# Query, key and leftover-row events of a fused attention and expert kernel, moved to other steps, and one of four row copies dropped

## The chip, the cores and the metric

One core of one Trainium2 chip runs the whole program in one launch. The metric is the device time of that core in microseconds (us). Three runs of the kernel before took 1332.02, 1334.98 and 1339.14 us; the median is 1334.98.

## The reference, cut to what matters

```python
def sm(a, b):                       # softmax of scale * a @ b.T over the last axis
    ...
a2k = sm(agents, k); agent_v = a2k @ v          # 49 agents, 4 batches of 11456 tokens, 128 wide
q2a = sm(q, agents); x = q2a @ agent_v          # one row per token
logits = x @ w_gate; expert_idx = argmax(logits)
gate_w = softmax(logits)[expert_idx]
for e in range(8):                              # 128 -> 1024 -> 128
    out[mask_e] = gate_w * (relu(x[mask_e] @ w1[e]) @ w2[e])
```

All inputs and the output are float32.

## The kernel before, in words

The four batches go one after the other. A batch has 11 chunks of 1024 tokens and one of 192, and every chunk has two groups of 512 tokens (the last one has one), 23 groups in all. For each batch the expert that most tokens choose is computed for all tokens, densely: 23 groups times 8 slices of the 1024 hidden values are 184 **steps**. The tokens of other experts are done in gathered blocks, late in the last batch and behind it.

A token's row x is never formed in the dense part. x is E times AV, with E the 49 exponentials of the token and AV the 49 agent values, so the first layer is E times (AV times w1). `esplit` (lines 581 to 588) writes each E as float16 parts into 128 columns of `mm`: 49 high parts, 49 low parts (E minus the high part), and the first 30 high parts once more. `eturn` (L593) turns that by a DMA transpose issued by SyncE into M, where those 128 columns are partitions. The weights W (L734) hold, for the first 98 rows, the high part of AV times w1, and for the last 30 rows its low part. 19 low-part rows (E 30 to 48) don't fit into 128; `rest` (L602) copies the 19 high-part partitions 30 to 48 of M four times into the tile Q, at partitions 0, 32, 64 and 96, and the weights Wq hold their low parts at the same places. A step of the first layer is thus two matmuls into one PSUM bank: L1190 (19 rows, from Q; four steps' worth are issued together, one per group of partitions) and L1198 (128 rows, from M). ScalarE then takes the relu in float16 (L1203) and VectorE its low part (L1204), and five steps later TensorE does the second layer, 12 matmuls a step (L1217). After the eighth slice VectorE scales the group by its factor (L1230, tile yo), and SyncE stores it.

The order of work is written out by a planner. `at(t, f)` puts a call at a time t in steps (`base` is 184 times the batch) and `after(dt, f)` puts one dt behind the present one; all calls are made in the order of these times, and each engine's instructions are in the order in which the calls made them. Nothing waits for the time itself; an engine that is ahead goes on. So the times set the order within each engine's queue, SyncE's (SP's) DMA queue among them, and waits come from data and buffers alone. The names that the change touches:

- Keys: chunk c of a batch is loaded, squared (L321), scaled and split into two float16 parts (L337, L339) from time `ks + 10 c` with ks = -208, its scores come 9 steps later. For batch 1 that is step -24 of batch 0 for c = 0. `KS1` is a list of such times for batch 1 alone, empty before.
- Queries: chunk c starts at `QA + 8 c` for c below 3 and then every 13 steps (`QC`; 10.5 in the last batch), with QA = -20. Batch 0's chunks have times of their own (`QS0`, `Q0`). Scores (`qscores`) follow 9 steps later (`KL`; 11 in the last batch from chunk 3), with the exponentials (`qexp`, L578); `esplit` 3 steps after the scores, `eturn` 0.5 after that (`DTE`), `rest` 3.5 after the turn (`DTQ`); `logits` (L610, the gate's logits, read from M) `LL` = 9.5 steps after the scores (`LLL` = 11 in the last batch).
- Each chunk c is used by the first layer from step 16 c on. M has 6 buffers, Q 3, yo 3, and a split key or query has two transposed buffers (hT, L361).
- Stores: `DEX` = 2 is the delay of the store of the exponentials behind `qexp`, `DST` = 2 that of the store of yo behind L1230.

Of the kernel before, what the change touches and what calls it, by code (L numbers as in the profile page):

```python
# [17 lines left out]
ALU = mybir.AluOpType  # L18
# [4 lines left out]
A = 49  # L23
KR = 128 - 2 * A
CH = 1024
BIG = float(1 << 20)
# [22 lines left out]
KS, KT, VT, VL, VL4, TW0, TW1, DW = -208, 10, 4, 4, 4, 8, 2.5, 1  # L49
QA, QB, QC, QB3, KL, LL, RG, D1, DL = -20, 8, 13, 10.5, 9, 9.5, 0.7, 0.5, 0  # L50

KS1 = []

KLL, LLL = 11, 11

DTR, DTE, DTQ, DEX, DST, DXS = 2, 0.5, 3.5, 2, 2, 0.5

# [13 lines left out]
def agent_moe_kernel(ctx, tc, q, k, v, agents, wg, w1, w2, out):  # L71
# [52 lines left out]
    nc.gpsimd.iota(itmp[:, 0:1], pattern=[[0, 1]], base=0, channel_multiplier=1)  # L124
    nc.vector.tensor_copy(pidx, itmp[:, 0:1])
    sumrow = cpool.tile([P, 1], F32, name="sumrow")
    nc.vector.tensor_scalar(sumrow, pidx, float(2 * A), None, op0=ALU.is_lt)
    restrow = cpool.tile([P, 1], F32, name="restrow")
    nc.vector.tensor_scalar(restrow, pidx, float(2 * A), None, op0=ALU.is_ge)
    eidx = cpool.tile([P, E], F32, name="eidx")  # L130
# [129 lines left out]
    def attention(b):  # L260
# [227 lines left out]
        def agentvalues(i):  # L488
# [10 lines left out]
            elif i == 2:  # L499
# [4 lines left out]
                nc.tensor.matmul(pt[:, :A], AV["acc"][:64 + A], both[:64 + A], start=True, stop=True)  # L504
                nc.vector.tensor_tensor(av[:, :2 * A].rearrange("p (j a) -> p j a", a=A), pt[:, :A].unsqueeze(1).broadcast_to([P, 2, A]),
                                        rs.unsqueeze(1).broadcast_to([P, 2, A]), op=ALU.mult)
                nc.vector.tensor_copy(av[:, 2 * A:], av[:, :KR])
                avq = one.tile([P, 4, 32], F32, tag="avq", name="avq")
# [72 lines left out]
        def esplit(c):  # L581
            _, p, t = chunks[c]
            e, m2 = Es[c], mm[c % len(mm)]
            nc.vector.tensor_copy(m2[:p, :t, :A], e[:p, :t, :])  # L584
            nc.scalar.copy(m2[:p, :t, 2 * A:], e[:p, :t, :KR])
            eng = nc.gpsimd if pick(M2L if last else M2E, c) == "P" else nc.vector
            eng.tensor_tensor(m2[:p, :t, A:2 * A], e[:p, :t, :], m2[:p, :t, :A], op=ALU.subtract)  # L587
            after(0 if first and c == 0 else DTE, eturn, c, m2)

        def eturn(c, m2):  # L590
            _, p, t = chunks[c]
            m = mpool.tile([P, 8, P], F16, tag="M", name="M")
            nc.sync.dma_start_transpose(m[:, :t, :p], m2[:p, :t, :].rearrange("p t a -> p (t a)"))  # L593
            Ms[c] = m
            after(0 if first and c == 0 else DTQ, rest, c)

        def rest(c):

            _, p, t = chunks[c]
            x = Qs[c] = mpool.tile([P, 8, P], F16, tag="Q", name="Q", bufs=MQ)  # L600
            for r in range(4):
                nc.sync.dma_start(x[32 * r:32 * r + A - KR, :t, :p], Ms[c][KR:A, :t, :p])  # L602

# [191 lines left out]
        for c in range(NCK):  # L795
# [11 lines left out]
            tl = max(t + ql_ + (TL if first and c < NQ else LLL if last and c > 2 else LL), ta + (TLM if first else 4) + c / 2)  # L807
            at(base + tl, logits, c)
            if c + 1 in starts or c == NCK - 1:
                turns(route(c), base + tl + 1, RG, 6)  # L810
# [364 lines left out]
    def experts(b):  # L1175
# [7 lines left out]
        def rests(g, f0):  # L1183
# [3 lines left out]
            for r in range(4):  # L1187
                k = slice(32 * r, 32 * r + A - KR)
                ph = phs[g, f0 + r] = psH.tile([P, 512], F32, tag="h", name="ph")
                nc.tensor.matmul(ph[:, :nn], st['Wq'][k, f0 // 4, :], st['Q'][c][k, h:h + n, :chunks[c][1]], start=True, stop=False)  # L1190

# [174 lines left out]
```

## Time and profile before

| | |
|---|---|
| runs, median (lowest to highest) | 1334.98 us (1332.02 to 1339.14) |
| profiled execution | 1331.0 us, span 1329.3 us |
| mean granted TensorE clock | 0.889 |
| TensorE (PE) busy | 1066.8 us, 80% of the span |
| VectorE (DVE) busy | 993.6 us, 75% |
| ScalarE (ACT) busy | 767.5 us, 58% |
| GpSimd (POOL) busy | 141.7 us, 11% |
| DMA queue of SP and ACT | 267792 packets, 192.36 MB, 63.5% of 16 engines' span |

The span is the time from the first to the last instruction of the profiled execution. Busy shares are means over the start (0 to 112 us), four batches of dense steps (112 to 1268 us) and the gathered blocks behind them. Weight loads (PEld) overlap matmuls. A granted clock of 1.0 is 2.4 GHz, of 0.5 it is 1.2 GHz.

### The profile page before, as it was taken

The page shows a single profiled execution, that of the slowest core. Times are in us where ns is not written, and L with a number is a line of the kernel's source. Part 1 is how long each engine was busy: PE and PEld are TensorE (multiplying, and loading weights), DVE is VectorE, ACT ScalarE, POOL GpSimd, SP SyncE. Part 2 cuts the span into 40 slices and gives each one's busy share as a digit, 9 for nine tenths or more (in the row PEclk, how much of TensorE's full clock was granted, in tenths as well). Part 3 has the DMA queues.
Part 4 walks back from the last instruction along what each step waited for, and adds up shares of the span by engine and source line. Part 5 has one row for each costly group of instructions (what it writes and reads, how often), then busy time and mean ns, then how long its engine had stood idle before and what let it go on. Part 6 is the DMA issues. An engine that isn't in the chain of part 4 may idle for free. (4 is left out here: it accounts for less than half of the span.)

```text
span 1329.3 us, 35044 instructions
## 1 busy us (share of the span) xinstructions
PE 1066.8 (80%) x14238; PEld 831.8 (63%) x14238; DVE 993.6 (75%) x2454; ACT 767.5 (58%) x1393; POOL 141.7 (11%) x198
## 2 busy tenths in 40 slices
PE   8626779789978668789987759779987859989995
PEld 8514657667765456567765547567765637666795
DVE  3677857678887768388886858497886957988975
ACT  4457745565586655365495745365483535665582
POOL 0200000032000000030200000030200102210123
PEclk9767988889988879799988988899987979888998
DMA  8679998643398999553298999733275456444170
GB/s 320 208 168 202 221 198 149 101 134 78 114 252 159 187 188 162 144 144 81 92 268 152 175 206 129 182 101 79 90 175 83 75 128 141 88 136 133 52 245 15
DMA packets 269813, 197.94 MB, mean 149 GB/s; under 512 B 218313, under 2 KB 231106, under 8 KB 269648
## 3 DMA queue, kind: packets, MB, share of 16 engines
q1 hardware_dynamic: 267792, 192.36, 63.5%
q0 software_dynamic: 1568, 2.25, 0.9%
q8 instruction: 113, 1.85, 0.6%
q10 hardware_dynamic: 288, 1.05, 0.2%
q14 instruction: 52, 0.43, 0.1%
HBM read 99.75 MB, written 36.43 MB: 102 GB/s over the span
## 5 line engine op out<-in xcount | busy, mean ns | idle before, releaser
L1217 PE MATMUL py<-w2h,hh 128*128 128x128 f16 (+1 forms) x5760 | 612.8, 230 | 31.1 <-DVE yo L1230 23.3
L1217 PEld LDWEIGHTS <-hh 128*128 128x128 f16 x8640 | 571.3, 104 | 102.7 <-issue 45.8
L1204 DVE SCALAR_TENSOR_TENSOR hh<-ph,hh 128x512 f16<-128x512 f32 (+1 forms) x736 | 479.3, 668 | 157.0 <-ACT hh L1203 152.9
L1203 ACT ACTIVATE hh<-ph 128x512 f16<-128x512 f32 (+1 forms) x728 | 405.5, 585 | 329.3 <-PE ph L1198 231.1
L1217 PE MATMUL py<-w2l,hh 128*128 128x128 f16 (+1 forms) x2880 | 554.3, 230 | 0.0
L1198 PE MATMUL ph<-M,W 128*128 128x512 f16 (+1 forms) x736 | 267.5, 397 | 0.0
L1190 PE MATMUL ph<-Q,Wq 19*128 19x512 f16 (+1 forms) x736 | 114.8, 399 | 67.3 <-DVE hh L1204 55.5
L1198 PEld LDWEIGHTS <-W 128*128 128x128 f16 x736 | 66.8, 99 | 126.5 <-issue 120.0
L321 ACT ACTIVATE jk<-ld 128x1024 f16<-128x1024 f32 (+1 forms) x84 | 84.7, 1009 | 49.0 <-DMA ld<-in_q_dram 37.7
L339 DVE SCALAR_TENSOR_TENSOR hl<-ld,mul,hl 128x1024 f16<-128x1024 f32 (+1 forms) x84 | 102.5, 1225 | 11.4 <-ACT hl L337 11.2
L337 ACT ACTIVATE hl<-ld,mul 128x1024 f16<-128x1024 f32 (+1 forms) x84 | 90.2, 1100 | 27.6 <-DVE mul L206 14.9
L610 PE MATMUL ps_small<-Gs,M 128*128 128x18 f16 x360 | 16.9, 173 | 95.5 <-DMA M<-mm 94.3
L388 PE MATMUL ps_small<-agh,hT 128*128 128x49 f16 (+1 forms) x630 | 64.6, 192 | 22.5 <-DMA hT<-hl 22.3
L587 POOL TENSOR_TENSOR mm<-E,mm 128x392 f16<-128x392 f32 (+1 forms) x18 | 15.6, 868 | 623.8 <-DVE mm L584 472.7
L610 PEld LDWEIGHTS <-M 128*128 128x128 f16 x360 | 13.6, 100 | 101.9 <-DMA M<-mm 100.0
L388 PEld LDWEIGHTS <-hT 128*128 128x128 f16 (+1 forms) x630 | 56.9, 102 | 27.3 <-DMA hT<-hl 23.3
L1190 PEld LDWEIGHTS <-Wq 19*128 19x128 f16 x736 | 25.6, 92 | 66.9 <-issue 50.3
L1230 DVE TENSOR_TENSOR yo<-py,cs 128x512 f32<-128x512 f32 (+1 forms) x92 | 61.4, 667 | 5.4 <-PE py L1217 5.3
L389 PE MATMUL ps_small<-agl,hT 128*128 128x49 f16 (+1 forms) x630 | 63.9, 191 | 0.0
L390 PE MATMUL ps_small<-agh,hT 128*128 128x49 f16 (+1 forms) x630 | 63.8, 191 | 0.0
L389 PEld LDWEIGHTS <-hT 128*128 128x128 f16 (+1 forms) x630 | 56.1, 102 | 7.2 <-issue 5.0
L390 PEld LDWEIGHTS <-hT 128*128 128x128 f16 (+1 forms) x630 | 55.4, 102 | 0.0
(295 smaller groups left out, 1309.7 us busy)
## 6 DMA issues: line engine op xcount, KB each, us to landing
ld<-in_k_dram SPq DMA_DIRECT2D x44, 512.0 KB
ld<-in_v_dram SPq DMA_DIRECT2D x44, 512.0 KB
ld<-in_q_dram SPq DMA_DIRECT2D x44, 512.0 KB
out_dram<-yo SPq DMA_DIRECT2D x88, 256.0 KB
w1e<-in_moe_w_dram SPq DMA_DIRECT2D x17, 512.0 KB
w2e<-in_moe_w_dram SPq DMA_DIRECT2D x17, 512.0 KB
exps<-E SPq DMA_DIRECT2D x44, 196.0 KB
wn<-in_moe_w_dram SPq DMA_DIRECT2D x16, 512.0 KB
```

What stands on the lines that cost most here:

```text
L321: nc.scalar.activation(jk[:p, :t * D], x[:p, :t, :].rearrange("p t d -> p (t d)"), AF.Square, accum_out=ss[:p])
L337: nc.scalar.activation(hi[:p, :t, :], x[:p, :t, :], AF.Copy, scale=m)
L339: nc.vector.scalar_tensor_tensor(lo[:p, :t, :], x[:p, :t, :], m, hi[:p, :t, :], op0=ALU.mult, op1=ALU.subtract)
L388: nc.tensor.matmul(o, x[:, 0, i, :p], AG["h"], start=True, stop=False)
L389: nc.tensor.matmul(o, x[:, 0, i, :p], AG["l"], start=False, stop=False)
L390: nc.tensor.matmul(o, x[:, 1, i, :p], AG["h"], start=False, stop=True)
L1190: nc.tensor.matmul(ph[:, :nn], st['Wq'][k, f0 // 4, :], st['Q'][c][k, h:h + n, :chunks[c][1]], start=True, stop=False)
L1198: nc.tensor.matmul(ph[:, :nn], st['W'][:, f, :], st['M'][c][:, h:h + n, :chunks[c][1]], start=False, stop=True)
L1203: nc.scalar.activation(hh[:, 0, :nn], ph[:, :nn], AF.Relu)
L1204: nc.vector.scalar_tensor_tensor(hh[:, 1, :nn], ph[:, :nn], 0.0, hh[:, 0, :nn], op0=ALU.max, op1=ALU.subtract)
L1217: mm_ = lambda l, r, **k: nc.tensor.matmul(o, l, r, skip_group_check=True, **k)
L1230: nc.vector.tensor_tensor(yo[:p, :n, :], py[:p, :n * D].rearrange("p (i d) -> p i d", d=D), cs.unsqueeze(2).broadcast_to([p, n, D]), op=AL ...
```

## The change

- The 128 columns of `mm` are laid out anew: 49 low parts, the first 17 high parts, all 49 high parts (columns 66 to 114), and 13 more high parts (17 to 29). The high parts 30 to 48 thus lie at partitions 96 to 114 of M. `av`, the row masks and the two ScalarE casts of `esplit` follow that layout.
- `rest` makes three copies in place of four, from partitions 96 to 114; the fourth of the L1190 matmuls reads M there. `rest` is no longer called behind `eturn` but from the plan, at `16 c - QD` with QD = 9, or at 6.5 steps behind the scores if that is later.
- QA goes from -20 to -26, LL from 9.5 to 14, LLL from 11 to 15; DEX from 2 to 4 and DST from 2 to 5.
- Batch 1's keys have times of their own: chunk c at step 3 + 7.6 c of batch 0.

```diff
--- before.py
+++ after.py
@@ -22,6 +22,8 @@
 P = 128
 A = 49
 KR = 128 - 2 * A
+UP = 96 - KR
+DUP = ((A, 0, UP - A), (UP + A, UP - A, KR))
 CH = 1024
 BIG = float(1 << 20)
 UNROLL = 4
@@ -47,13 +49,13 @@
 VE, T1, TF0, TF1, TL, TLM, Q0 = 12, 1.75, 3, 1.5, 18, 10, 2
 
 KS, KT, VT, VL, VL4, TW0, TW1, DW = -208, 10, 4, 4, 4, 8, 2.5, 1
-QA, QB, QC, QB3, KL, LL, RG, D1, DL = -20, 8, 13, 10.5, 9, 9.5, 0.7, 0.5, 0
-
-KS1 = []
-
-KLL, LLL = 11, 11
-
-DTR, DTE, DTQ, DEX, DST, DXS = 2, 0.5, 3.5, 2, 2, 0.5
+QA, QB, QC, QB3, KL, LL, RG, D1, DL = -26, 8, 13, 10.5, 9, 14, 0.7, 0.5, 0
+
+KS1 = [3 + 7.6 * c for c in range(12)]
+
+KLL, LLL = 11, 15
+
+DTR, DTE, QD, DEX, DST, DXS = 2, 0.5, 9, 4, 5, 0.5
 
 LAG = 5
 
@@ -123,10 +125,14 @@
     pidx = cpool.tile([P, 1], F32, name="pidx")
     nc.gpsimd.iota(itmp[:, 0:1], pattern=[[0, 1]], base=0, channel_multiplier=1)
     nc.vector.tensor_copy(pidx, itmp[:, 0:1])
+    restrow = cpool.tile([P, 1], F32, name="restrow")
+    for o, a0, a1 in DUP:
+        nc.vector.tensor_scalar(itmp[:, 1:2].bitcast(F32), pidx, float(o), None, op0=ALU.is_ge)
+        nc.vector.tensor_scalar(itmp[:, 2:3].bitcast(F32), pidx, float(o + a1 - a0), None, op0=ALU.is_ge)
+        nc.vector.tensor_tensor(itmp[:, 3 + (a0 > 0):4 + (a0 > 0)].bitcast(F32), itmp[:, 1:2].bitcast(F32), itmp[:, 2:3].bitcast(F32), op=ALU.subtract)
+    nc.vector.tensor_tensor(restrow, itmp[:, 3:4].bitcast(F32), itmp[:, 4:5].bitcast(F32), op=ALU.add)
     sumrow = cpool.tile([P, 1], F32, name="sumrow")
-    nc.vector.tensor_scalar(sumrow, pidx, float(2 * A), None, op0=ALU.is_lt)
-    restrow = cpool.tile([P, 1], F32, name="restrow")
-    nc.vector.tensor_scalar(restrow, pidx, float(2 * A), None, op0=ALU.is_ge)
+    nc.vector.tensor_scalar(sumrow, restrow, -1.0, 1.0, op0=ALU.mult, op1=ALU.add)
     eidx = cpool.tile([P, E], F32, name="eidx")
     itmp2 = cpool.tile([P, E], I32, name="itmp2")
     nc.gpsimd.iota(itmp2, pattern=[[1, E]], base=0, channel_multiplier=0)
@@ -502,9 +508,10 @@
                 av = wpool.tile([P, P], F32, tag="av", name="av")
                 pt = small_ps()
                 nc.tensor.matmul(pt[:, :A], AV["acc"][:64 + A], both[:64 + A], start=True, stop=True)
-                nc.vector.tensor_tensor(av[:, :2 * A].rearrange("p (j a) -> p j a", a=A), pt[:, :A].unsqueeze(1).broadcast_to([P, 2, A]),
-                                        rs.unsqueeze(1).broadcast_to([P, 2, A]), op=ALU.mult)
-                nc.vector.tensor_copy(av[:, 2 * A:], av[:, :KR])
+                nc.vector.tensor_tensor(av[:, :A], pt[:, :A], rs, op=ALU.mult)
+                nc.vector.tensor_copy(av[:, UP:UP + A], av[:, :A])
+                for o, a0, a1 in DUP:
+                    nc.vector.tensor_copy(av[:, o:o + a1 - a0], av[:, a0:a1])
                 avq = one.tile([P, 4, 32], F32, tag="avq", name="avq")
                 nc.gpsimd.memset(avq, 0.0)
                 nc.gpsimd.tensor_copy(avq[:, :, :A - KR], av[:, KR:A].unsqueeze(1).broadcast_to([P, 4, A - KR]))
@@ -581,10 +588,12 @@
         def esplit(c):
             _, p, t = chunks[c]
             e, m2 = Es[c], mm[c % len(mm)]
-            nc.vector.tensor_copy(m2[:p, :t, :A], e[:p, :t, :])
-            nc.scalar.copy(m2[:p, :t, 2 * A:], e[:p, :t, :KR])
+            up = m2[:p, :t, UP:UP + A]
+            nc.vector.tensor_copy(up, e[:p, :t, :])
+            for o, a0, a1 in DUP:
+                nc.scalar.copy(m2[:p, :t, o:o + a1 - a0], e[:p, :t, a0:a1])
             eng = nc.gpsimd if pick(M2L if last else M2E, c) == "P" else nc.vector
-            eng.tensor_tensor(m2[:p, :t, A:2 * A], e[:p, :t, :], m2[:p, :t, :A], op=ALU.subtract)
+            eng.tensor_tensor(m2[:p, :t, :A], e[:p, :t, :], up, op=ALU.subtract)
             after(0 if first and c == 0 else DTE, eturn, c, m2)
 
         def eturn(c, m2):
@@ -592,14 +601,13 @@
             m = mpool.tile([P, 8, P], F16, tag="M", name="M")
             nc.sync.dma_start_transpose(m[:, :t, :p], m2[:p, :t, :].rearrange("p t a -> p (t a)"))
             Ms[c] = m
-            after(0 if first and c == 0 else DTQ, rest, c)
 
         def rest(c):
 
             _, p, t = chunks[c]
             x = Qs[c] = mpool.tile([P, 8, P], F16, tag="Q", name="Q", bufs=MQ)
-            for r in range(4):
-                nc.sync.dma_start(x[32 * r:32 * r + A - KR, :t, :p], Ms[c][KR:A, :t, :p])
+            for r in range(3):
+                nc.sync.dma_start(x[32 * r:32 * r + A - KR, :t, :p], Ms[c][96:96 + A - KR, :t, :p])
 
         def logits(c):
             _, p, t = chunks[c]
@@ -806,6 +814,7 @@
             at(base + t + ql_ + 3, esplit, c)
             tl = max(t + ql_ + (TL if first and c < NQ else LLL if last and c > 2 else LL), ta + (TLM if first else 4) + c / 2)
             at(base + tl, logits, c)
+            at(base + max(c * 16 - QD, t + ql_ + 6.5), rest, c)
             if c + 1 in starts or c == NCK - 1:
                 turns(route(c), base + tl + 1, RG, 6)
                 tf = max(tl + 1 + 6 * RG, tw + 1)
@@ -1187,7 +1196,8 @@
             for r in range(4):
                 k = slice(32 * r, 32 * r + A - KR)
                 ph = phs[g, f0 + r] = psH.tile([P, 512], F32, tag="h", name="ph")
-                nc.tensor.matmul(ph[:, :nn], st['Wq'][k, f0 // 4, :], st['Q'][c][k, h:h + n, :chunks[c][1]], start=True, stop=False)
+                nc.tensor.matmul(ph[:, :nn], st['Wq'][k, f0 // 4, :], st['Q' if r < 3 else 'M'][c][k, h:h + n, :chunks[c][1]],
+                                 start=True, stop=False)
 
         def layer1(g, f):
             c, h, n = groups[g]
```

## Rows read from the trace of the kernel before

**Rows 1.** Busy time by stretch (us from the span's start and length; busy us of PE, PEld, DVE, ACT and POOL with their instructions; granted clock; DMA share and GB/s). Batch 0's chunks 0 to 6 run from 112 to 295; batch 1's chunks 0 to 7 from 400 to 618 and the rest of it to 701; batch 2's chunks 0 to 7 from 701 to 919.

```profile
112.00:295.00 183.00, 148.45 (x2029) 113.45 (x2026) 133.91 (x282) 111.39 (x204) 16.51 (x15) 0.87 0.83 172
...
400.00:618.00 218.00, 170.66 (x2362) 129.60 (x2362) 159.41 (x362) 127.13 (x233) 16.17 (x17) 0.88 0.77 159
618.00:701.00 83.00, 74.26 (x1015) 57.55 (x1014) 68.86 (x187) 54.17 (x97) 10.90 (x28) 0.96 0.55 155
701.00:919.00 218.00, 169.42 (x2361) 128.90 (x2361) 158.46 (x362) 124.70 (x226) 16.20 (x17) 0.89 0.79 152
```

**Rows 2.** What TensorE waited for between the first and the last step, 112 to 1268 us (us in total, times, longest us).

```profile
PE ps_small L610 <- DMA M<-mm: 86.2, 21, 8.2
PE ph L1190 <- DVE hh L1204: 55.5, 39, 11.3
PE py L1217 <- DVE yo L1230: 23.3, 28, 2.9
PE ph L1190 <- DMA Q<-M: 9.9, 11, 2.0
```

**Rows 3.** TensorE in order of time before the first step (start us, us, instruction, count, and in brackets the idle time before it and what ended it).

```profile
91.78 0.38 PE L610 MATMUL ps_small<-Gs,M 128*128 128x18 f16 x8 [1.05 <-DMA M<-mm]
...
107.80 0.22 PE L388 MATMUL ps_small<-agh,hT 128*128 128x49 f16 x1 [14.95 <-DMA hT<-hl]
...
111.68 0.61 PE L1190 MATMUL ph<-Q,Wq 19*128 19x512 f16 x4
```

**Rows 4.** SP's DMA queue in order of time before the first step (start us, us until the last of the group was issued).

```profile
87.51 2.09 SPq L593 DMA_TRANSPOSE M<-mm  x1
...
90.36 5.58 SPq L602 DMA_DIRECT2D Q<-M  x8
96.04 11.77 SPq L361 DMA_TRANSPOSE hT<-hl  x2
```

**Rows 5.** Groups of instructions by line over the whole span (count, busy us, mean ns of one, idle before).

```profile
L339 DVE SCALAR_TENSOR_TENSOR hl<-ld,mul,hl 128x1024 f16<-128x1024 f32 (+1 forms) x84 | 102.5, 1225 | 11.4 <-ACT hl L337 11.2
L337 ACT ACTIVATE hl<-ld,mul 128x1024 f16<-128x1024 f32 (+1 forms) x84 | 90.2, 1100 | 27.6 <-DVE mul L206 14.9 <-DMA hT<-hl 12.7
L321 ACT ACTIVATE jk<-ld 128x1024 f16<-128x1024 f32 (+1 forms) x84 | 84.7, 1009 | 49.0 <-DMA ld<-in_q_dram 37.7 <-DVE hb L202 6.0 <-DMA ld<-in_k_dram 4.9
```

**Rows 6.** SP's queue in order of time at the start of batch 1.

```profile
396.14 2.53 SPq L602 DMA_DIRECT2D Q<-M  x4
```

**Rows 7.** TensorE in order of time at the start of batch 1, the first-layer lines.

```profile
400.15 0.37 PE L1190 MATMUL ph<-Q,Wq 19*128 19x512 f16 x1 [0.44 <-DMA Q<-M]
...
401.90 0.37 PE L1190 MATMUL ph<-Q,Wq 19*128 19x512 f16 x1 [1.00 <-DMA Q<-M]
...
403.46 0.58 PE L1190 MATMUL ph<-Q,Wq 19*128 19x512 f16 x1 [0.87 <-DMA Q<-M]
```

**Rows 8.** SP's queue in order of time around the transpose of M of batch 1's chunk 4.

```profile
464.09 1.24 SPq L593 DMA_TRANSPOSE M<-mm  x1
465.43 3.76 SPq L361 DMA_TRANSPOSE hT<-hl  x1
469.29 2.46 SPq L602 DMA_DIRECT2D Q<-M  x4
```

**Rows 9.** The first layer's L1198, one matmul a step, from the span's start to 464.09 us: count; shortest, median and longest ns; start of the first and the last; forms. The same 228 stand there up to 468.5 us.

```profile
L1198 PE MATMUL ph<-M,W x228: 243/379/634, 112.2 to 461.0; 128*128 128x512 f16 x110, 128*128 128x192 f16 x4
```

**Rows 10.** TensorE in order of time, the logits of two chunks of batch 1.

```profile
468.76 0.38 PE L610 MATMUL ps_small<-Gs,M 128*128 128x18 f16 x8 [7.37 <-DMA M<-mm]
...
537.37 0.38 PE L610 MATMUL ps_small<-Gs,M 128*128 128x18 f16 x8 [8.22 <-DMA M<-mm]
```

**Rows 11.** What TensorE waited for from 112 to 295 us (batch 0).

```profile
PE ph L1190 <- DVE hh L1204: 15.0, 5, 5.9
PE ps_small L610 <- DMA M<-mm: 11.2, 4, 5.4
PE py L1217 <- DVE yo L1230: 8.1, 6, 2.9
```

**Rows 12.** What TensorE waited for from 400 to 618 us (batch 1).

```profile
PE ps_small L610 <- DMA M<-mm: 30.4, 5, 8.2
PE py L1217 <- DVE yo L1230: 5.1, 4, 2.7
PE ph L1190 <- DVE hh L1204: 4.6, 6, 2.0
```

**Rows 13.** Busy time by short stretches in batch 1, columns as in rows 1. Packets are booked by their start, so a share can pass 1.

```profile
452.00:468.00 16.00, 8.75 (x129) 6.36 (x126) 10.37 (x15) 9.99 (x20) 0.00 (x0) 0.88 0.99 236
468.00:474.00 6.00, 5.24 (x56) 5.24 (x57) 2.22 (x6) 1.79 (x3) 0.00 (x0) 0.50 0.55 137
474.00:494.00 20.00, 13.59 (x217) 10.73 (x215) 15.47 (x32) 12.56 (x22) 0.90 (x1) 0.93 1.08 205
494.00:499.00 5.00, 4.62 (x48) 2.81 (x49) 3.27 (x7) 2.91 (x7) 0.00 (x0) 0.50 0.56 145
```

**Rows 14.** What SP waited for from 400 to 618 us (us in total, times, longest us).

```profile
SPq L602 <- DMA M<-mm: 6.3, 4, 3.3
...
SPq L1293 <- DVE yo L1230: 3.5, 2, 2.5
```

**Rows 15.** The casts of L585 over the whole span (count; shortest, median and longest ns; start of the first and the last; forms).

```profile
L585 ACT CAST mm<-E x48: 230/387/467, 74.8 to 1164.4; 128x240 f16<-128x240 f32 x44, 96x60 f16<-96x60 f32 x4
```

## The prediction, made before the change was run

> **What bounds the kernel now.** I read the stretches first [rows 1]. Steps run at two paces. In the last third of a batch TensorE is busy nearly throughout; in the first two thirds (400 to 618 us for the second batch, 128 steps, so 1.7 us a step) it is busy 171 of 218 us at a mean granted clock of 0.88, VectorE 159, and the DMA engines 0.77 of the time: no engine is full, so something in the order of the work makes holes. The waits of TensorE name it [rows 2]: of its idle time from step 0 to the last step 86.2 us, in 21 waits, go to the logits (L610) for the transposed chunk M; the next ones are 55.5 us for VectorE's hh, 23.3 us for yo, 9.9 us for Q. The third thing to see is the start: TensorE ends the first batch's logits at 92.2 us, and its first layer matmul starts at 111.68 us; the 14.95 us before 107.80 are a wait for a key transpose of the *second* batch, which stands ahead of the first layer in its program [rows 3].
>
> **The change part by part.** The sum is made against the profiled execution, 1331.0 us (span 1329.3); the median of the runs shown is 1334.98, 4 us above it, and I add those 4 us at the end.
>
> *Second batch's keys (KS1).* Key chunks 0, 1 and 2 of batch 1 were due at steps -24, -14 and -4, with scores nine steps later; they are now due at 3, 10.6 and 18.2, so no key stands ahead of the first layer. What is late next? M of chunk 2 is issued at 87.51 to 89.60 [rows 4], its logits start at 91.78 [rows 3], and the first three Q copies, now due at step -9, come behind that transpose on SP. Four copies took 2.53 us to issue at a batch's start [rows 6], so three take 1.9: 89.7 to 91.6. There the first copy's user ran 4.0 us after the issue began (396.14 to 400.15) [rows 6, 7], so the first layer can start near 95.6 instead of 111.7: **-16**. Bounds: -19.5 (straight behind the logits, 92.2) and -10 (the copies stuck behind one more hT transpose: the two at 96.04 held SP 11.77 us, some 6 each).
>
> The three chunks' work now lies beside steps 3 to 30: VectorE 3 x 1.2 for L339, ScalarE 3 x (1.0 + 1.1) for L321 and L337 [rows 5], and three loads and transposes on DMA. At no cost if holes hide it; fully serial it is three hT transposes of about 5.9 us of SP, some 17 us [rows 4]. The first batch's dense stretch already runs at DMA 0.83 [rows 1], so I take a bit under half: **+8**, bounds 0 and +17.
>
> *Queries six steps sooner, logits later (QA, LL, LLL).* QA moves the queries of batches 1 to 3 by -6, LL adds 4.5: logits come 1.5 steps sooner than before, but M's turn (esplit + 0.5) comes 6 sooner, so the lead from M's issue to its use grows from 6 to 10.5 steps. (In batch 0 only the logits move, later.) Example: chunk 4 of batch 1 has M due at step 184 + 34.5; SP issued it at 464.09 [rows 8], when TensorE had done 228 steps [rows 9], 9.5 steps late; it was in use at 468.76, after a wait of 7.37 us [rows 10]. 4.5 steps at the free pace of some 1.2 us are 5.4 us. The longest of the 21 waits are 8.22 and 7.37 [rows 10]; cutting 5.4 from each leaves some 10 us in all, so 76 go. But a wait that goes is not a time that goes. In batch 0's dense stretch M waits are only 11.2 us, and there hh and yo hold TensorE 23.1 us; in batch 1's M holds it 30.4, and those two 9.7 [rows 11, 12]. 19.2 us less of the one goes with 13.4 more of the others, in stretches with different work; I take the nearer middle, 0.6 of 76: **-46**. Bounds 0 (all replaced) and -86 (all gone).
>
> A cross-check by the engine that is fullest there: 0.77 x 218 is 168 us of DMA; packed to 0.87 it would need 193, 25 less in each of batches 1 and 2, with a few more in the others. The same size.
>
> *The clock.* After the wait of 7.37 us that ended at 468.76 [rows 10], the granted clock is 0.50 (1.2 GHz) from 468 to 474, with TensorE busy 5.24 of 6.00 us; from 474 to 494 it is 0.93 [rows 13]. The Trainium skill (TensorE: Matmul & The Clock Gate, "HAM oscillation — how this bites in real kernels") tells of the same: a kernel that waits on DMA in every round of its loop starts each round with a cold array. By that rule the forecast here is too small, since each wait that goes also gives back part of a half-speed stretch. I leave it out of the sum (whoever replaces M may keep the holes), and it is the second rival below.
>
> *Q copies (three, nine steps ahead).* Before, a chunk's four copies were due 3.5 steps after M's issue, and SP stood waiting for M (6.3 us in 400 to 618) [rows 14]. At the three later batch starts Q was due 4 steps ahead; it is now 9: of the 9.9 us of Q waits [rows 2] **-7** (bounds 0, -9.9). At all other chunk starts Q used to be there long before its use; now it has 9 steps, at 1.5 us some 13.5 us. From the first issue to the third group's start took 7.3 us at a batch start (396.14 to 403.46) [rows 6, 7]. So SP may run about 4 steps late before TensorE waits; the example's Q was due at step 222 and issued at 228 [rows 8, 9], 6 late, so 2 steps or 3 us of wait is possible at the worst chunks, numbers 2 to 7 of each batch, 24 in all. I take a seventh of that: **+10**, bounds 0 and +72. The fourth copy's issue, 48 x 0.6 us of SP, goes beside other work: 0 (bounds 0, -5); the fourth group now reads partitions 96 to 114 of M, which its partner matmul reads anyway.
>
> *Stores later (DST, DEX).* SP's waits for yo are short where it is tight, 3.5 us in 400 to 618 [rows 14]; elsewhere nothing urgent stands behind them. 0, bounds -10 and 0; yo has three buffers for one store every eight steps, so five steps of delay fit.
>
> *Layout of the split.* ScalarE's one cast of 240 elements (0.39 us; 60 elements took 0.23) becomes two of 136 and 104: by that line 0.30 + 0.27, so 0.2 more in each of 45 chunks [rows 15], 9 us of an engine busy 127 of 218 [rows 1]; hidden, **+0**, bound +9. Two more small VectorE copies in each batch's av and six more small operations at the program's start, beside the key loads: **+1**, bounds 0 and +3.
>
> Sum: -16 + 8 - 46 - 7 + 10 + 1 = **-50**, 1281 us for the profiled execution, 1285 as a median.
>
> **Rivals.**
> *Given back* (chance 0.18): in the dense stretches DMA or SP is the bound, and M's wait is where it shows. For it: DMA stands at 0.99 to 1.08 (packets booked by their start) at 452 to 468 and 474 to 494; against: it falls to 0.55 between them, right after TensorE's wait for M, and to 0.56 behind them [rows 13]. Then 16 of the start remain, against up to 17 for the three key chunks, and the edges' 7: 0 to -15, 1320 to 1335. The Trainium skill (Perfetto Trace Analysis, "What \"DMA-bound\" means") puts such a bound on the DMA engines or on the issuing sequencer, and only fewer or larger descriptors help it; here that would be one copy in four alone. The holes in the DMA share speak against it.
> *More* (0.10): all M waits go and nothing follows, and the clock stays up: -16 - 86 - 7 and 2.6 us (half of 5.24) [rows 13] after half of the 21 waits, 27: -136 + 8, some 1207.
> *Slower* (0.12): the Q copies come late. The place is L1190 at each chunk's start, where nothing waited before. The 9 steps allow a lag of 4; at M's 9.5 it would cost 5.5 steps, 8 us, in each of 24 chunks, far more than all gains. It turns the change into a loss from 60 us in all, 2.5 us a chunk, a mean lag of near 6 steps, which the example's Q just had. The price I give it is +10 to +30: 1345 to 1365. Against it: a shorter queue lags less, since SP no longer stands for M.
> That the change doesn't do what it says would show at the start alone: if layer 1 still waited there, -16 would be missing; it is within the first rival.
>
> **How the numbers follow.** Forecast (-15 to -90) 0.60, given back 0.18, more 0.10, slower 0.12. A measurement of this kernel can tell about 0.5%, 6.7 us, from no change. Faster by over that: 0.60 + 0.10 + 0.10 of the first rival: 0.80; within it 0.08 of that rival and 0.02 of the last: 0.10; slower 0.10. The range 1245 to 1331 holds the forecast and most of the first rival and leaves out the last and most of "more", some 0.2.
>
> **What would show it.** Start: the first L1190 at 93 to 98 us, behind a Q copy. Keys: chunks 0 to 7 of batch 0 no more than about 10 us longer. M: waits of L610 between first and last step under 25 us. Q: L1190 waiting for Q between 5 and 20 us in all; over 50 and the last rival is right. If M's waits go and the 400 to 618 stretch is not shorter, while hh and yo waits grow by as much, the factor 0.6 was wrong. A granted clock above 0.93 in that stretch would mean that the clock's share was wrongly left out.

## The result, and the profile after

The changed kernel took 1263.18 us (median; 1261.11 the lowest) against 1336.72 for the kernel before in the same sitting: ratio 0.9449, 95% interval 0.9411 to 0.9486, some 73 us less. The forecast was 1285. The profiled execution took 1261.11 us with a span of 1259.4, against 1331.0 and 1329.3. Some executions of any of these kernels take 17 to 38 us more, nearly all of it in the first 66 us where a profile shows one: medians are of all executions, ratios and the times of single runs of the others alone, and of the kernels with the keys alone and the queries alone, profiled in such an execution, only what lies behind the start is read.

The page of the changed kernel, the engines (busy us, share of the span, instructions), and the DMA queue of SP and ACT (packets, MB, share of 16 engines):

```profile
PE 1059.1 (84%) x14238; PEld 821.6 (65%) x14238; DVE 986.2 (78%) x2468; ACT 767.1 (61%) x1441; POOL 139.6 (11%) x198
q1 hardware_dynamic: 266756, 190.62, 63.5%
```

The work is the same to within 8 us on each engine (11 in the weight loads); what went is for the most part holes. Where, a table of the two spans shows (us; the start goes to the first step, the "first eight" are chunks 0 to 7 of the four batches together, "the others" the rest of each batch, with the edge to the next):

| kernel | start | first eight | the others | behind the last batch's steps | span |
|---|---|---|---|---|---|
| before | 112.2 | 838.6 | 317.2 | 61.3 | 1329.3 |
| after | 89.4 | 802.5 | 308.7 | 58.8 | 1259.4 |

So 22.8 us went at the start, 36.1 in the dense two thirds of the batches, 8.5 in the other third, 2.5 behind it. The busy time by stretch of the changed kernel, columns as in [rows 1]; the lines are batch 0's, 1's and 2's chunks 0 to 7:

```profile
89.40:290.70 201.30, 170.45 (x2370) 128.12 (x2366) 160.82 (x368) 133.07 (x250) 18.09 (x17) 0.89 0.88 186
371.60:577.30 205.70, 170.92 (x2360) 129.66 (x2356) 159.00 (x359) 129.51 (x248) 15.84 (x17) 0.90 0.79 172
662.00:865.70 203.70, 170.73 (x2360) 128.77 (x2357) 159.42 (x359) 126.09 (x239) 15.46 (x17) 0.90 0.78 165
```

Batches 1 and 2 have the same busy time of TensorE in 206 and 204 us as before in 218 [rows 1]: 12 and 15 us of holes less, at a granted clock of 0.90 against 0.88 and 0.89. TensorE's waits from the first step to the last (us in total, times, longest), to be read beside [rows 2]:

```profile
PE ph L1199 <- DVE hh L1214: 42.6, 56, 2.7
PE ps_small L618 <- DMA M<-mm: 35.0, 9, 6.2
PE ps_small L394 <- DMA hT<-hl: 27.7, 8, 8.5
PE py L1227 <- DVE yo L1240: 23.3, 28, 4.1
```

(L1199, L618 and L394 are before's L1190, L610 and L388.) The wait for M fell from 86.2 to 35.0, that for Q from 9.9 to nothing, and a new one stands third: the scores wait for the transposed keys and queries (hT), which cost 1.5 us before. The start, TensorE and then SP in order of time:

```profile
88.52 0.38 PE L618 MATMUL ps_small<-Gs,M 128*128 128x18 f16 x8 [5.30 <-DMA M<-mm]
88.83 0.61 PE L1199 MATMUL ph<-Q,Wq 19*128 19x512 f16 x3
```

```profile
72.51 1.29 SPq L602 DMA_TRANSPOSE M<-mm  x1
...
75.83 0.74 SPq L610 DMA_DIRECT2D Q<-M  x1
...
81.69 1.23 SPq L610 DMA_DIRECT2D Q<-M  x2
83.05 1.27 SPq L602 DMA_TRANSPOSE M<-mm  x1
84.41 2.01 SPq L610 DMA_DIRECT2D Q<-M  x3
```

The first layer starts straight behind chunk 2's logits, at 88.83 us. No key stands ahead of it, and its copies stand at 75.83 and 81.69, before M of chunk 2 in SP's queue and not behind it as the prediction had it. They stood before it in the kernel before, too (M of chunk 0, chunk 0's copies, M of chunk 1):

```profile
76.20 1.24 SPq L593 DMA_TRANSPOSE M<-mm  x1
...
79.28 3.02 SPq L602 DMA_DIRECT2D Q<-M  x4
...
82.92 3.28 SPq L593 DMA_TRANSPOSE M<-mm  x1
```

What came sooner by itself is M: 72.51 against 76.20 for chunk 0, 83.05 against 87.51 [rows 4] for chunk 2, and with it the logits.

### The profile page after: what moved, and what is told of

Same layout as the page of the kernel before. It is cut to its first block, busy times and chain, and to the rows that moved or that the text cites. A ratio compares the mean times of both kernels' runs of the same rounds, so it can differ in the third digit from the quotient of the medians.

```text
span 1259.4 us, 35046 instructions
## 1 busy us (share of the span) xinstructions
PE 1059.1 (84%) x14238; PEld 821.6 (65%) x14238; DVE 986.2 (78%) x2468; ACT 767.1 (61%) x1441; POOL 139.6 (11%) x198
## 4 chain that ended last, share of the span: by engine, by line
PE 42%; DVE 18%; DMA 16%; ACT 9%; issue 9%; SPq 3%; POOL 2%; another core or an unknown queue 1%; POOLq 0%; ACTq 0%; DVEq 0%
PE py L1227 23%; DVE hh L1214 7%; PE ph L1208 7%; DMA hT<-hl 5%; ACT hh L1213 4%; DMA wn<-in_moe_w_dram 3%; PE ph L1199 3%; DMA M<-mm 3%; DVE hl L345 2%; DMA ld<-in_q_dram 2%; PE ps_small L484 2%; ACT hl L343 2%; DVE S L456 2%; PE ps_small L392 2%; DVE yo L1240 2%
## 5 line engine op out<-in xcount | busy, mean ns | idle before, releaser
L1227 PE MATMUL py<-w2h,hh 128*128 128x128 f16 (+1 forms) x5760 | 602.8, 228 | 27.7 <-DVE yo L1240 23.3
L1227 PEld LDWEIGHTS <-hh 128*128 128x128 f16 x8640 | 560.8, 103 | 97.4 <-issue 49.0
L1208 PE MATMUL ph<-M,W 128*128 128x512 f16 (+1 forms) x736 | 259.7, 391 | 0.2 <-issue 0.2
L1208 PEld LDWEIGHTS <-W 128*128 128x128 f16 x736 | 67.0, 100 | 119.3 <-issue 110.8
L1199 PE MATMUL ph<-Q,Wq 19*128 19x512 f16 (+1 forms) x552 | 99.4, 390 | 26.0 <-DVE hh L1214 20.0
L327 ACT ACTIVATE jk<-ld 128x1024 f16<-128x1024 f32 x84 | 85.2, 1014 | 47.1 <-DMA ld<-in_q_dram 31.1
L345 DVE SCALAR_TENSOR_TENSOR hl<-ld,mul,hl 128x1024 f16<-128x1024 f32 x84 | 101.0, 1208 | 5.1 <-ACT hl L343 4.7
L343 ACT ACTIVATE hl<-ld,mul 128x1024 f16<-128x1024 f32 x84 | 90.9, 1105 | 9.7 <-DVE mul L212 6.4
L1199 PE MATMUL ph<-M,Wq 19*128 19x512 f16 (+1 forms) x184 | 72.0, 391 | 26.3 <-DVE hh L1214 22.6
L394 PE MATMUL ps_small<-agh,hT 128*128 128x49 f16 x630 | 61.9, 188 | 30.0 <-DMA hT<-hl 29.5
L394 PEld LDWEIGHTS <-hT 128*128 128x128 f16 x630 | 54.1, 100 | 38.0 <-DMA hT<-hl 33.3
L1199 PEld LDWEIGHTS <-Wq 19*128 19x128 f16 x736 | 27.4, 91 | 64.5 <-issue 38.4
L395 PE MATMUL ps_small<-agl,hT 128*128 128x49 f16 x630 | 61.6, 188 | 0.0
L396 PE MATMUL ps_small<-agh,hT 128*128 128x49 f16 x630 | 61.6, 188 | 0.0
L395 PEld LDWEIGHTS <-hT 128*128 128x128 f16 x630 | 53.2, 100 | 6.2 <-issue 3.4
L618 PE MATMUL ps_small<-Gs,M 128*128 128x18 f16 x360 | 16.8, 172 | 45.8 <-DMA M<-mm 43.8
L396 PEld LDWEIGHTS <-hT 128*128 128x128 f16 x630 | 52.9, 99 | 0.0
```

The source lines that it names most:

```text
L327: nc.scalar.activation(jk[:p, :t * D], x[:p, :t, :].rearrange("p t d -> p (t d)"), AF.Square, accum_out=ss[:p])
L343: nc.scalar.activation(hi[:p, :t, :], x[:p, :t, :], AF.Copy, scale=m)
L345: nc.vector.scalar_tensor_tensor(lo[:p, :t, :], x[:p, :t, :], m, hi[:p, :t, :], op0=ALU.mult, op1=ALU.subtract)
L394: nc.tensor.matmul(o, x[:, 0, i, :p], AG["h"], start=True, stop=False)
L395: nc.tensor.matmul(o, x[:, 0, i, :p], AG["l"], start=False, stop=False)
L396: nc.tensor.matmul(o, x[:, 1, i, :p], AG["h"], start=False, stop=True)
```

## The experiments

The total came out near the forecast, but by which terms? The theory was the prediction's: the queries' lead brings most (-46), the start about 8 net, the copies nothing. The rival: the copies or the transposes' queue bring it, and the lead little.

**One part taken out of the changed kernel.** Four runs, each with one part as before.

```diff
-KS1 = [3 + 7.6 * c for c in range(12)]
+KS1 = []
```

> The changed kernel with KS1 empty again, so batch 1's keys stand ahead of the first layer as before. My theory (the start is worth about what the trace shows there, 22.9 us, and the three key chunks hide in batch 0): the first layer matmul again near 112 us, 1263 + 15 to + 23 = 1278 to 1286. Rival (the moved keys are paid for later, so the start is given back): within 5 us of 1263, with batch 0's chunks 0 to 7 shorter by as much as the start is longer.

Measured: 1266.54 us, ratio 0.9523 (0.9464 to 0.9582) against the change's 0.9449 (0.9411 to 0.9486). The first step comes at 109.8 us, 20.4 later; chunks 0 to 7 of the four batches take 786.7 us, 15.8 less than in the changed kernel, and TensorE's waits for M and hT are shorter (those for hh are 4.9 us longer, 47.5):

```profile
PE ps_small L618 <- DMA M<-mm: 25.9, 7, 6.2
PE ps_small L394 <- DMA hT<-hl: 22.0, 6, 8.2
```

So the keys win 20 us at the start and most of it is lost among the steps; 3 (by medians) to 10 us (by ratios) are left, and as the two ratios' intervals overlap, it is not shown that anything is. The loss lies where neither theory put it: of the 15.8 us only 2.8 are in batch 0 (201.4 us against 198.6), beside which the keys' work now lies, and 9.7 in the last batch (191.7 against 182.0). That last stretch took 182.9 us in the run with the old stores below as well, so it may follow from the order of the work and not from the keys; this stays open.

```diff
-QA, QB, QC, QB3, KL, LL, RG, D1, DL = -26, 8, 13, 10.5, 9, 14, 0.7, 0.5, 0
+QA, QB, QC, QB3, KL, LL, RG, D1, DL = -20, 8, 13, 10.5, 9, 9.5, 0.7, 0.5, 0
-KLL, LLL = 11, 15
+KLL, LLL = 11, 11
```

> The changed kernel with QA = -20, LL = 9.5, LLL = 11 again. My theory (the lead from M's issue to its logits makes the M waits): waits of L618 for M between first and last step back from 35 us to 70 to 90, time 1263 + 20 to + 40 = 1283 to 1303. Rival (SP's queue, freed of copies that waited for M, made M early): those waits stay under 50 us and the time within 8 us of 1263.

Measured: 1282.15 us, ratio 0.9627 (0.9598 to 0.9656): 0.0178 above the change, 24 us (19 by medians). Its waits:

```profile
PE ps_small L618 <- DMA M<-mm: 73.4, 20, 10.1
PE ph L1199 <- DVE hh L1214: 39.1, 35, 8.7
PE py L1227 <- DVE yo L1240: 26.1, 28, 4.3
PE ps_small L394 <- DMA hT<-hl: 9.6, 4, 4.0
PE ph L1199 <- DMA Q<-M: 8.9, 9, 2.2
```

The wait for M is back, and yet the kernel is some 50 us faster than the one before. The lead is not what most of the gain comes from. The waits for Q are back as well, though the copies' rule stayed new: at the batch starts it is bound to the scores, and with the old queries gives 4.5 steps ahead and not 9.

```diff
         Ms[c] = m
+        after(0 if first and c == 0 else 3.5, rest, c)
...
-            at(base + max(c * 16 - QD, t + ql_ + 6.5), rest, c)
```

> The changed kernel with its three copies issued 3.5 steps behind M's turn, as before, in place of nine steps ahead of use. My theory (worth the 9.9 us of Q waits and a little of SP's waiting for M): 1263 + 5 to + 12 = 1268 to 1275, Q waits of 5 to 10 us at the batch starts. Rival (a copy that waits for M, or for one of Q's three buffers, holds SP's whole queue, and that was most of what the batches lost): + 20 or more, with M and hT waits both longer.

Measured: 1254.19 us, ratio 0.9397 (0.9355 to 0.944), below what either side had expected, and no wait for Q. The copies' new time brings nothing; whether it costs the 7 us between the two ratios is taken up below.

```diff
-DTR, DTE, QD, DEX, DST, DXS = 2, 0.5, 9, 4, 5, 0.5
+DTR, DTE, QD, DEX, DST, DXS = 2, 0.5, 9, 2, 2, 0.5
```

> The changed kernel with DEX = 2 and DST = 2 again. My theory (SP's waits for yo lie where nothing urgent is behind them): within 5 us of 1263. Rival (the later stores unblock SP): + 10 us or more, with SP's waits for yo and for the exponentials longer in the first two thirds of a batch and M waits up.

Measured: 1261.99 us, ratio 0.9475 (0.9447 to 0.9503). The stores' delay is worth nothing that can be measured.

**One part put into the kernel before.** None of the four explains 40 us of the gain; what all four kept is the column layout with its three copies. So each of the three remaining parts was tried alone, and the copies due three steps ahead of use in place of nine.

```diff
-KS1 = []
+KS1 = [3 + 7.6 * c for c in range(12)]
```

> The kernel before with KS1 of the changed kernel alone. My theory: the first layer starts 14 to 20 us sooner (the four Q copies are then on its path), and some 5 us are paid back in batch 0: 1337 - 8 to - 18 = 1319 to 1329. Rival (given back): within 5 us of 1337.

Measured: 1332.75 us in a single run, no ratio. Chunks 0 to 7 of batch 0 take 217.3 us against 203.7, those of the last batch 210.1 against 200.2, and TensorE waits 103.3 us for M against 86.2 [rows 2]. One run can't carry a size; 13.6 us lost in batch 0 are to be seen.

```diff
-QA, QB, QC, QB3, KL, LL, RG, D1, DL = -20, 8, 13, 10.5, 9, 9.5, 0.7, 0.5, 0
+QA, QB, QC, QB3, KL, LL, RG, D1, DL = -26, 8, 13, 10.5, 9, 14, 0.7, 0.5, 0
-KLL, LLL = 11, 11
+KLL, LLL = 11, 15
```

> The kernel before with QA = -26, LL = 14, LLL = 15 alone. The Q copies then come six steps sooner too, right behind M. My theory (the lead removes the M waits, hT and hh take part of it): L610's waits for M from 86 us to 25 to 45, time 1337 - 20 to - 40 = 1297 to 1317. Rival (SP still stands at the Q copies, so M and the hT behind them stay late): M waits over 60 us and the time within 10 us of 1337.

Measured: ratio 0.9801 (0.9731 to 0.9872), some 27 us. Its waits:

```profile
PE ph L1190 <- DVE hh L1204: 46.8, 50, 6.8
PE ps_small L388 <- DMA hT<-hl: 30.4, 7, 6.1
PE py L1217 <- DVE yo L1230: 26.9, 33, 3.2
PE ps_small L610 <- DMA M<-mm: 18.3, 8, 5.1
```

Of M's 86.2 us 68 went, and 29 came back as a wait of the scores for hT (1.5 us before); none is for Q. That is the wait that takes the place of M's, and the prediction had not named it.

```diff
-            for r in range(4):
-                nc.sync.dma_start(x[32 * r:32 * r + A - KR, :t, :p], Ms[c][KR:A, :t, :p])
+            for r in range(3):
+                nc.sync.dma_start(x[32 * r:32 * r + A - KR, :t, :p], Ms[c][96:96 + A - KR, :t, :p])
...
-... st['Q'][c][k, h:h + n, :chunks[c][1]] ...
+... st['Q' if r < 3 else 'M'][c][k, h:h + n, :chunks[c][1]] ...
```

(with the layout of `esplit`, `av` and the masks that belongs to it, and the copies called behind the transpose as before)

> The layout and the three copies of the changed kernel with all times of the kernel before (copies 3.5 steps behind M's turn, QA = -20, LL = 9.5, LLL = 11, DEX = 2, DST = 2, no KS1). My theory (29 us of SP issue and one copy of four were hidden): 1337 - 6 to + 3 = 1331 to 1340. Rival (SP's issue time is the bound in the dense stretches): 1337 - 15 or more.

Measured: 1298.16 and 1290.5 us in two single runs, no ratio, some 40 us below the kernel before. The part priced at nothing is the largest.

```diff
-DTR, DTE, QD, DEX, DST, DXS = 2, 0.5, 9, 4, 5, 0.5
+DTR, DTE, QD, DEX, DST, DXS = 2, 0.5, 3, 4, 5, 0.5
```

> The changed kernel with the copies three steps ahead of use in place of nine (QD = 3). It measures the rival that I gave the slower side to. If SP lags by about as much as it did (3 to 6 steps), L1199 waits for Q at nearly every chunk start, some 3 to 8 us each: waits for Q of 50 us or more and 1263 + 25 or more. If SP hardly lags now: Q waits under 20 us and within 10 us of 1263.

Measured: 1263.11 us, ratio 0.9432 (0.9352 to 0.9512), and no wait for Q among TensorE's. But the edit did not make the copies late. Batch 1's chunk 5, in the changed kernel and then with this edit: M's transpose, the copies, and the first layer's L1208, one matmul a step, from the batch's first step to the copies' issue (count; shortest, median and longest ns; start of the first and the last; forms).

```profile
451.28 1.51 SPq L602 DMA_TRANSPOSE M<-mm  x1
...
456.39 1.86 SPq L610 DMA_DIRECT2D Q<-M  x3
L1208 PE MATMUL ph<-M,W x52: 376/379/390, 371.6 to 451.7; 128*128 128x512 f16 x52
```

```profile
452.60 1.52 SPq L602 DMA_TRANSPOSE M<-mm  x1
...
457.58 1.86 SPq L610 DMA_DIRECT2D Q<-M  x3
L1208 PE MATMUL ph<-M,W x52: 376/379/390, 374.1 to 453.9; 128*128 128x512 f16 x52
```

52 steps had begun and the chunk is used from step 80 on, so the copies are issued 28 steps ahead in both, not 9 or 3. They come right behind their own M, ahead of M of chunk 6 (475.35 us in the changed kernel), which the plan puts at step 54.5 (the query at 42, scores 9 later, `esplit` 3, the turn 0.5) and these copies at 71. So SP's queue does not keep the plan's order here, unlike what the description of the kernel says; what moves the copies forward is not shown. In both kernels every chunk's copies but those of batch 0's first are issued 8 to 36 steps ahead of use. The rival of late copies falls because no copy came late; what late copies would cost, this run doesn't show, and `QD` hardly acts.

**Is it the copy or the layout?** Two kernels separate them; a third and a control look at the copies' time again. All four stood in one sitting.

```diff
-            for r in range(3):
+            for r in range(4):
...
-... st['Q' if r < 3 else 'M'][c][k, h:h + n, :chunks[c][1]] ...
+... st['Q'][c][k, h:h + n, :chunks[c][1]] ...
```

(on top of the layout alone)

> The kernel before with the change's column layout alone, and all four row copies kept: the fourth group of the 19-row matmuls reads the tile Q again, whose fourth group is copied from partitions 96 to 114 of M like the other three. The layout with three copies took about 1293 us in its undisturbed runs, 40 us less than before. Theory A, the fourth copy costs that (48 issues and their short packets in a DMA queue where the transposes stand behind them): the time goes back to 1335, within 8 us; TensorE's waits for M are 80 to 92 us again, and SP's time in the transposes of queries and keys (hT) in chunks 0 to 7 of batches 0 to 2 is 75 to 86 us each. Theory B, it is the layout (source partitions 96 to 114 in place of 30 to 48, or the two smaller casts): 1293, within 8, M waits 60 to 70, hT 63 to 74 us. In between, both have a part.

Measured: 1345.63 us, ratio 1.0074 (1.0045 to 1.0104): the whole gain is gone, and 10 us more, 2.6 us beyond theory A's bound.

```diff
-            for r in range(4):
+            for r in range(3):
...
-... st['Q'][c][k, h:h + n, :chunks[c][1]] ...
+... st['Q' if r < 3 else 'M'][c][k, h:h + n, :chunks[c][1]] ...
```

(on the kernel before, its layout kept)

> The kernel before in its old column layout, with three row copies in place of four; the fourth group's 19-row matmul reads partitions 96 to 114 of M, which in this layout are other rows, so in every fourth slice the low-part correction of 19 rows is taken with the wrong rows: that part of the computation is changed, the amount of work is not. Theory A (the fourth copy is the cost): 1293 us, within 8, M waits 60 to 70 us, hT transposes on SP 63 to 74 us in chunks 0 to 7 of batches 0 to 2. Theory B (the layout is): 1335, within 8, M waits 80 to 92, hT 75 to 86.

Measured: 1298.94 us, ratio 0.9704 (0.9674 to 0.9734). One copy less, in the old layout, is 39 us; taken out of the new layout it is about 50 (1345.63 to 1290.5 and 1298.16). By the times theory A holds. Its signs for four copies come near, those for three fail: the waits for M are 79.2 us with four copies in the new layout and 76.0 with three in the old (80 to 92 and 60 to 70 expected), and SP's time in hT transposes, in chunks 0 to 7 of batches 0 to 2, is 79, 89 and 85 us against 76, 82 and 81 (75 to 86 and 63 to 74 expected). The gain stands in all of TensorE's idle time from the first step to the last, and in its clock. Length, and then TensorE's busy time and granted clock, in the stretch of all steps, in the old layout with four copies and with three:

```profile
112.20:1268.10 1155.90, 961.08 (x12882) 733.16 (x12878) 888.64 (x2176) 680.52 (x1249) 112.28 (x160) 0.90 0.65 143
107.90:1233.40 1125.50, 949.80 (x12881) 724.91 (x12878) 888.82 (x2175) 680.87 (x1249) 112.41 (x160) 0.91 0.64 145
```

and in the new layout with four and with three:

```profile
111.30:1279.80 1168.50, 969.89 (x12882) 736.03 (x12878) 889.92 (x2182) 684.11 (x1294) 112.50 (x160) 0.89 0.64 141
111.50:1237.20 1125.70, 953.79 (x12882) 730.09 (x12878) 886.73 (x2183) 682.40 (x1295) 114.19 (x160) 0.91 0.63 145
```

In the old layout 30.4 us went, 11.3 of them busy time of the same number of matmuls, at a mean granted clock of 0.91 against 0.90, and 19.1 idle time (194.8 to 175.7). In the new one 42.8 went, 16.1 busy, at 0.91 against 0.89, and 26.7 idle. In these traces the granted clock stands at 0.5 or at 1.0 (1.2 or 2.4 GHz), and a mean in between tells how long it stood at each. The waits for M, hh and hT shrank by 10.2, 10.5 and -1.4 us in the old layout and by 12.9, 1.1 and 5.1 in the new: no one wait carries it.

*What a copy costs.* Nothing near its issue of 0.6 us alone. The kernel before, batch 1, SP's queue in order of time and then the DMA engines in the 7.6 us that follow (each digit is the busy share of all 16 engines, in tenths, in one fortieth of the window):

```profile
444.64 2.45 SPq L602 DMA_DIRECT2D Q<-M  x4
447.20 6.19 SPq L361 DMA_TRANSPOSE hT<-hl  x1
...
469.29 2.46 SPq L602 DMA_DIRECT2D Q<-M  x4
471.85 0.39 SPq L1293 DMA_DIRECT2D out_dram<-yo  x1
472.29 6.20 SPq L361 DMA_TRANSPOSE hT<-hl  x1
```

```profile
DMA  0000100000000000101344799999000000000000
GB/s 0 11 11 22 22 0 0 32 22 22 11 11 32 22 22 22 11 11 47 77 51 65 121 140 140 150 88 47 32 22 32 22 22 32 22 22 32 22 22 15
DMA packets 586, 0.29 MB, mean 38 GB/s; under 512 B 510, under 2 KB 510, under 8 KB 586
```

586 less 510 are 76 packets of 2 KB: four copies times 19 partitions. They fill nearly the whole window, 11 to 32 GB/s, one to three packets in most slices of 0.19 us, 7.3 us in all or 0.096 us a packet: one after another, as on a single engine, while the share of the 16 reads 0. A copy so takes 1.8 us. The transpose issued at 447.20 stands among them: its short packets (the hump of nines) begin to move, stop, and SP is let go at 453.39, just behind the last packet of the copies. Where no copies stand ahead, a transpose of hT held SP for 3.76 us [rows 8]; with four copies just ahead 6.19 and 6.20 here. The mean of all hT transposes that SP began within 1 us of the last copy, from 112 us on, is 6.24 us (11 of them) with four copies, and 5.08 (10) with three in the old layout; those of the kernel before with no copy within 4 us ahead took 2.85 (67, some of them of short chunks). The run with the layout alone has the same place at 435 us, with three copies; its engines from 436.0 to 442.3 us:

```profile
DMA  0000001000001004100013479779999928400000
GB/s 0 0 0 26 13 0 13 13 26 13 13 26 13 13 26 78 29 29 26 26 28 89 78 102 114 93 127 141 114 39 44 41 29 29 15 26 26 13 26 18
DMA packets 573, 0.25 MB, mean 39 GB/s; under 512 B 516, under 2 KB 516, under 8 KB 573
```

573 less 516 are 57, three times 19, in single file again. So a fourth copy is 1.8 us of a queue in which the transposes of keys, queries and M stand: by an estimate 44 chunks of 1024 tokens times 1.8 are 79 us, of which about half came back as time. SP's issue alone, 48 times 0.6 or 29 us, is less than the 39 that went, so it can't be all of it; no run takes the issue and the passage apart.

The Trainium skill (DMA: Bandwidth & Descriptors, "Why a DMA increments its semaphore by 16 and not by 1", under "How many engines") gives a reason: a copy is spread over the largest number of engines, up to 16, that divides the size of its slowest dimension on both sides, and 19 has no such divisor but 1. The trace agrees, at 0.096 us a packet, one behind the other. No run here made this copy with another number of partitions, so that 20 or 32 rows would go faster was not tried.

**The copies' time once more.**

```diff
-DTR, DTE, QD, DEX, DST, DXS = 2, 0.5, 9, 4, 5, 0.5
+DTR, DTE, QD, DEX, DST, DXS = 2, 0.5, 9, 2, 2, 0.5
...
         Ms[c] = m
+        after(0 if first and c == 0 else 3.5, rest, c)
...
-            at(base + max(c * 16 - QD, t + ql_ + 6.5), rest, c)
```

> The changed kernel with its row copies called 3.5 steps behind M's transpose again and the stores 2 steps behind their work, so that layout, three copies, keys and queries are what is left of the change. The row copies' old time alone took 1254 us against 1263, the old stores alone 1262. Theory A (the copies' new time costs some 8 us because the copies then fall among later transposes; the stores are nothing): 1254, within 4. Theory B (that difference was the spread from one schedule to the next): 1262, within 4.

> The changed kernel, unchanged, beside the others on one chip: 1262 us, within 4. It is the measure for the run with old copies and stores: if it is 1256 or less here, the 8 us of that theory are the spread between sittings.

Measured: 1262.97 us, ratio 0.9457 (0.9433 to 0.9481), beside the changed kernel's 1261.72, 0.9439 (0.9417 to 0.946). With the old stores the copies' old time is worth nothing. Old copies with the new stores gave 0.9397 (0.9355 to 0.944), the lowest of the study, and that interval overlaps with both of the changed kernel's; whether those 6 to 7 us are real stays open. The two times of the copies also differ little in the trace: batch 1's chunk 5 is issued 28 steps ahead of use with either of them and the new stores, 30 with either and the old.

## Why the prediction was right, and where it was not

*What was right.* The direction, and that the total, 1263, lies within 1245 to 1331. That is luck in good part: the largest term was put at 0 and measured -40, the next was put at -46 and measured -24 to -27, and the +10 set for late copies did not come.

*The step that failed: "The fourth copy's issue, 48 x 0.6 us of SP, goes beside other work: 0 (bounds 0, -5)".* It measured some -40 (39 in the old layout). The term counted SP's issue and not the copy's passage through the DMA engines, 1.8 us each in single file. It stood in the rows of the prediction: at batch 1's start the groups of L1190 began at 400.15, 401.90 and 403.46 [rows 7], 1.75 and 1.56 us apart, each waiting for its own copy, while all four had been issued within 2.53 us [rows 6]. And the low DMA shares of 0.55 and 0.56 [rows 13], taken to speak against DMA as the bound, do not: four copies are issued inside each of the two windows, at 469.29 [rows 8] and 494.39 us, and a queue behind one packet at a time looks nearly idle in the mean of 16. "One copy in four alone" was named under the first rival as the only thing that would help there, and the rival was given 0.18.

*M's waits, -46.* The queries' lead alone measured -24 (taken out of the change) to -27 (put into before). The mechanism was right: 68 us of M's wait went, and M's wait returns to 73.4 when the queries go back. The factor was 0.4 of the waits that went (27 of 68), not 0.6 of 76, as 29 us of the wait moved to hT, whose transposes stand in the same queue; the text looked only at hh and yo for the successor, and its own rows, 13.4 of 19.2 replaced, would have left 0.3. M stayed at 35.0 with a bound of 25 set for it.

*The start, -16 and +8 paid back.* The first layer came 22.9 us sooner, beyond the bound of 19.5. The sum put the copies behind M of chunk 2, since they are due at step -9; in both kernels chunk 0's copies stand ahead of it, so they were never on this path. And the bound took the logits' end, 92.2, as fixed: with the keys gone M of chunk 2 was issued 4.5 us sooner, and the logits begin at 88.52 against 91.78 [rows 3]. What is lost later is also larger, 10 to 17 us, as the run without the keys shows; net 3 to 10 against the 8 said. But the mechanism of +8, three chunks' work beside batch 0, shows only 2.8 us in the changed kernel; with keys alone batch 0 is 13.6 us longer, so the check "batch 0 no more than 10 us longer" would fail there and passes in the changed kernel (201.4 us, 2.4 shorter). That the missing copy makes the difference is likely, as it shortens batch 0 by 6.6 us in the old layout, but not tested with the keys in place.

*Q.* The 9.9 us at the batch starts went, as said (-7), but not by the copies' new time: they are gone with the queries' lead alone and with the copies at their old time, and 8.9 us of them are there with the new rule and the old queries. The new waits (+10) did not come, because the copies did not stand nine steps ahead but 8 to 36. With them the slower rival falls, without its case having been run.

*Stores, clock.* The stores are nothing, as said. The granted clock of batch 1's dense stretch is 0.90, under the mark of 0.93, so "more" did not come; but the clock's share was not nothing either: over the span it went from 0.889 to 0.913, and in the two pairs of runs on the copy the same matmuls take 11 of 30 and 16 of 43 us less.

The sum as measured: -40 for the copy, -24 to -27 for the queries, -3 to -10 for the keys, 0 for the rest: -67 to -77, against -73 measured. The new layout by itself, with four copies, is 10 us slower; with three it shows no such cost (1290.5 and 1298.16 us against 1290.98 to 1299.68 in the old layout). Why is open.

## What to carry to other kernels

Price a DMA by three things: its issue, how many engines carry it, and what stands behind it in the queue. A small copy can hold a queue for longer than its issue; look for a stretch in which the mean DMA share is near 0 while a transfer is still on its way, and count its packets against the time. Where a wait is shortened by lead, ask which other consumer of the same queue waits next: here lead took 68 us of waits away and 29 came back elsewhere. And look up in the trace where an event that was moved in the plan has gone, before its effect is priced or its run is read.

## What the runs showed of the hardware that was not expected

That transfers of 38 KB each can move one packet at a time, 1.8 us a transfer, while the mean share of the 16 DMA engines reads 0 to 0.1; and that a DMA transpose behind such copies holds SP too, not only its own data: 6.2 us behind four of them, where the one ahead of them took 3.8 [rows 8].
